# Attention and a gated feed-forward layer on one core: two more head pairs with an unsplit product with v

## The chip, the core and the metric

The kernel runs on one core of a Trainium2 chip. The metric is the device time of one execution in microseconds (us); the figure for a kernel is the median of its runs. The engines are TensorE (PE in the profile, PEld for its weight loads), VectorE (DVE), ScalarE (ACT), GpSimd (POOL) and SyncE (SP), which issues nearly all transfers.

## The reference

For each of 8 batches and 8 heads (576 positions, 64 channels per head) attention is computed with a threshold: scores more than tau below the maximum of their row are dropped. The output of the heads is then fed through two large matrices with a gate between them.

```python
scores = scale * np.matmul(q, k.transpose(0, 1, 3, 2))
thresh = np.max(scores, axis=-1, keepdims=True) - tau
scores = np.where(scores >= thresh, scores, -1000000000.0)
scores = scores - np.max(scores, axis=-1, keepdims=True)
attn = np.exp(scores)
attn = attn / (np.sum(attn, axis=-1, keepdims=True) + 1e-09)
out = np.matmul(attn, v)                 # all heads side by side: x, 4608 x 512
h = x @ w_in                             # 512 -> 2048
g = h * np.tanh(log1p(exp(h)))
return g @ w_out                         # 2048 -> 512
```

## The kernel before, in words

**Tiles, steps, pairs.** Two heads make a *pair*; there are 32 pairs, four to a batch. The 2 x 576 query rows of a pair are nine *tiles* of 128 rows, so there are 288 tiles, numbered g = 0 to 287 over all pairs. One main loop runs over g; a turn of it is called a *step* here. Each engine does its instructions in the order in which this loop writes them (class `InOrder`, whose call is line 93: nearly every row of the profile carries L93 for that reason). Only SP's transfers are ordered by the scheduler.

**What a step does.** In step g, PE computes the scores s of tile g+1 (`begin`). DVE takes the row maximum of tile g (`row_max`, a TENSOR_REDUCE), ACT the exponential e (`exponential`), DVE masks and sums to p (`masked`), POOL normalises p of tile g-1 (`normalise`). PE transposes p of tile g-2 into tp and t (`transposes`); ACT copies the transposed tile g-3 to SBUF. The product with v (`product`) is made once per group of tiles: a pair has four of them, closed by its tiles 1, 4, 6 and 8 (`LAST`), 256 or 320 columns wide; their result y goes to x by ACT (the *gather*). When a pair is done, `split_x` makes xh and xl of it.

**Split and plain.** A float32 product is made on PE either *plain* (operands float32) or *split*: an operand is rounded to the short form fp32r (hi) and the rest is kept as a second operand (lo), and two or three fast matmuls replace the slow one. Pairs below `FULL` (4) have the plain product with v: `values_full`, five chunks `y<-pf,vf` and one gather. Their transposed tiles are copied as they are (`evacuate`: pf), and they take a transposition of the tail t in every tile. Later pairs have the split one: `values`, nine matmuls with hi, lo and tk; ACT rounds tp to hi and the tail to tk, DVE subtracts (`lo_main`, `tail_lo`), POOL splits v, and after the product ACT copies two halves (x, yo), which POOL adds. The first four pairs also have plain scores for their second head (`PLAIN`), the others split scores for both.

**The bookkeeping of the two forms.** In the plain form the transposes of tile g-2 stand early in a step, after the scores, and a product comes four steps after the tile that closes it; its gather stands on ACT one step after its last chunk. In the split form the transposes stand at the end of a step, the product comes five steps after, and its gather stands in the same step. In the first 39 steps the chunks of a plain product are dealt out over steps (`PIECES`: 2 to 4 per step); from then on up to five are issued in a step.

**First matrix product.** From step 42 on PE also runs the product h with w_in of the batch before (`gemm1`), as a stream from which each step takes a written number of matmuls: `MIX_FIRST` for the first batch, beginning with 6, 14, 22, 6, 16, 4, 12, 4, 15, 9, 16, 13 for the steps 42 to 53. Twelve matmuls fill one PSUM bank, which ACT then copies out (`leave`, hst). Banks of h and banks of y come out of one pool of two (`psh`). w_in is decoded from 8-byte words while the first 53 steps run (`Decode`: dec on ACT, DVE and POOL; w1h, w1l). The second product (o) follows the attention.

Of the kernel before, what the change touches and what calls it, by code (L numbers as in the profile page):

```python
# [16 lines left out]
NP = H // 2  # L17
LOADS = ((1, 0, 1, 3, 2, 3, 7, 3, 5, 8), (0, 3, 3, 2, 5, 4, 5, 8, 5, 7), (0, 0, 2, 4, 5, 4, 7, 6, 7, 8))
# [5 lines left out]
ORDER = (0, 0)  # L24
PIECES = (3, 3, 3, 3, 4, 2, 3, 4, 3)
WARM = (24, 2, 10)
FULL = NP
UNV = 54
ONP = 1
ONV = (3, 9, 11, 12, 14, 15, 17, 18, 22)  # L30
# [1 line left out]
PLAIN = (1,)  # L32
# [46 lines left out]
def fv(ap):  # L79
    return ap.bitcast(F32)  # L80
# [78 lines left out]
def attention_moe(tc, q, k, v, tau, w_in, w_out, out):  # L159
# [3 lines left out]
    with ExitStack() as outer:  # L163
# [12 lines left out]
        with ExitStack() as first:  # L176
# [6 lines left out]
            with ExitStack() as att:  # L183
# [31 lines left out]

                def prep(pi):
                    full = pi < FULL
                    plain = PLAIN if full else ()
                    qs, k1, k2 = [], [], []
                    for a in range(2):  # L220
                        kind = F32 if a in plain else F32R
                        qs.append(ops.tile([P, 640], kind, name=f"q{a}"))
                        k1.append(ops.tile([P, S + D], kind, name=f"k1{a}"))
                        k2.append(None if a in plain else ops.tile([P, S + D], kind, name=f"k2{a}"))
                    made = dict(qs=qs, k1=k1, k2=k2, plain=plain)
                    if full:
                        made["vf"] = ops.tile([P, 2, 5, D], F32, name="vf", tag="vs")

                    def part(src, n):
                        r = raw.tile([P, 320], F32, name="r")  # L230
                        nc.sync.dma_start(r[:, :n], src)
                        return r[:, :n]

                    def q_part(c):
                        a, half = divmod(c, 2)
                        sl = slice(half * 320, (half + 1) * 320)
                        at = slice(c * 320, (c + 1) * 320)
                        if a in plain:
                            nc.sync.dma_start(qs[a][:D, sl], q[pi, :D, at])
                            return skip  # L240
                        r = part(q[pi, :, at], 320)

                        def split():
                            nc.scalar.copy(qs[a][:, sl], r)
                            nc.gpsimd.tensor_tensor(qs[a][D:, sl], r[D:], fv(qs[a][D:, sl]), ALU.subtract)

                        return split

                    def k_part(a, c):
                        sl = slice(c * 320, (c + 1) * 320)  # L250
                        if a in plain:
                            nc.sync.dma_start(k1[a][:D, sl], k[pi, :D, a, sl])
                            return skip
                        r = part(k[pi, :, a, sl], 320)

                        def split():
                            nc.scalar.copy(k1[a][:, sl], r)
                            nc.gpsimd.tensor_tensor(k2[a][:, sl], r, fv(k1[a][:, sl]), ALU.subtract)

                        return split  # L260

                    def v_part(a):
                        if full:
                            nc.sync.dma_start(made["vf"][:, a], v[pi, :, a])
                            return skip
                        if a == 0:
                            made["vs"] = ops.tile([P, 2, 5, 2, D], F32R, name="vs")
                        vs = made["vs"]
                        r = part(v[pi, :, a].rearrange("p c d -> p (c d)"), 320)
                        r = r.rearrange("p (c d) -> p c d", d=D)  # L270

                        def split():
                            nc.scalar.copy(vs[:, a, :, a, :], r)
                            nc.gpsimd.tensor_tensor(vs[:, a, :, 1 - a, :], r, fv(vs[:, a, :, a, :]), ALU.subtract)

                        return split

                    loads = [lambda c=c: q_part(c) for c in range(4)]
                    loads += [lambda a=a, c=c: k_part(a, c) for a in range(2) for c in range(2)]
                    loads += [lambda a=a: v_part(a) for a in range(2)]  # L280
                    return made, loads
# [49 lines left out]
                def transposes(g):  # L331
# [7 lines left out]
                    t5 = None  # L339
                    if g < FULL * 9:  # L340
                        t5 = pst.tile([P, P], F32, name="t5")
# [47 lines left out]
                def values_full(r, pt, vf, x):  # L389
                    main, tail = pt.pop(r)  # L390
                    n = WIDTH[r]
                    a = r // 2
                    y = psh.tile([P, 512], F32, name="y", tag="ph")

                    def chunk(c):
                        if c < 4:
                            nc.tensor.matmul(y[:D, :n], vf[:, a, c], main[:, c, :n], start=c == 0, stop=False)
                        else:
                            nc.tensor.matmul(y[:D, :n], vf[:D, a, 4], tail[:D, 0, :n], start=False, stop=True)

                    def gather():
                        nc.scalar.copy(x[a * D:a * D + D, XOFF[r]:XOFF[r] + n], y[:D, :n])

                    return [lambda c=c: chunk(c) for c in range(5)], gather
# [108 lines left out]
                def start_pair(g, pi):  # L513
                    parts, todo = prep(pi)
                    pairs[pi] = dict(ops=parts, pt={})
                    for work, step in zip(todo, LOADS[1 if 2 <= pi < FULL + 2 else pi % 2 * 2]):
                        loads.setdefault(g + step, []).append(work)

                def begin(g):
                    pi, t = divmod(g, 9)  # L520
                    made = pairs[pi]["ops"]
                    tiles[g] = dict(s=scores(t, D if g % 2 == 0 else 0, **made))

                def product(g):
# [4 lines left out]
                    if t in LAST:  # L529
                        if pi < FULL:  # L530
                            some, gather = values_full(LAST[t], pr["pt"], pr["ops"]["vf"], pr["x"])
# [14 lines left out]

                warm_up(WARM[0])
                start_pair(0, 0)
                for step in range(8):
                    for work in loads.pop(step, []):  # L550
                        work()()
                begin(0)
                for g in range(NT + 5):
                    now = [work.pop(0) for work in decoding]
                    decoding = [work for work in decoding if work]
                    if g + 1 < NT:
                        begin(g + 1)
                    ahead = 2 <= g < FULL * 9 + 2
                    lag = 4 if g < FULL * 9 + 4 else 5
                    if lag <= g < NT + lag and g != FULL * 9 + 4:  # L560
                        product(g - lag)
                    if 3 <= g < NT + 3:
                        old = ((g - 3) % 9, *tiles[g - 3]["tp"], pairs[(g - 3) // 9]["pt"])
                        full = g - 3 < FULL * 9
# [6 lines left out]
                        tiles[g - 2]["tp"] = transposes(g - 2)  # L571
                    done = list(ready)
                    ready.clear()
                    for _ in range(5 if g >= FULL * 9 + 3 else PIECES[g % 9]):
                        if pieces:
                            work, then = pieces.pop(0)
                            work()
                            if then:
                                ready.append(then)
# [39 lines left out]
                    if g % 9 == 7 and g // 9 + 2 < NPAIRS:  # L619
                        start_pair(g, g // 9 + 2)  # L620
                    if g == 0:
                        start_pair(-2, 1)
                        loads[0] = loads.pop(-2) + loads[0]
# [17 lines left out]
                    b, step = divmod(g - 6, 36)  # L641
# [54 lines left out]
            work = {}  # L696
# [139 lines left out]
        for c, ds, qs in steps:  # L836
# [3 lines left out]
            g = ready[c]  # L840
# [58 lines left out]
```

## Time and profile before

| | |
|---|---|
| runs | 1384.63, 1387.59, 1375.18 us (median 1384.63) |
| profiled execution | 1382.82 us, its span 1381.0 us |
| PE busy | 1360.2 us (98%) |
| DVE, ACT, POOL busy | 1000.4 (72%), 944.0 (68%), 771.9 us (56%) |
| step 36 begins on DVE, step 56 begins | 126.55 us, 199.60 us |
| first matmul of h | 149.14 us |

The times in the profile are counted from the start of the span. The first three slices of the 40 hold the first four pairs (plain), the next two hold pairs 4 and 5. A matmul's record is longer than the distance to the next one, since matmuls overlap in the engine; distances between starts are used below where work is counted.

### The profile page before, as it was taken

What the parts mean: (1) busy time and instruction counts of PE and PEld (TensorE: products, weight loads), DVE (VectorE), ACT (ScalarE), POOL (GpSimd) and SP (SyncE); (2) the same over time, 40 slices, a digit from 0 to 9 for tenths busy, and PEclk for the clock granted to TensorE, in tenths of its full rate; (3) what the DMA queues carried; (4) which work ended last, traced back from release to release, by engine and by line L of the source; (5) the groups of instructions that cost most, each with busy time, mean ns of one, the idle gap of its engine ahead of it and who ended that gap; (6) DMA issues with size and microseconds to landing.
All of it is one profiled execution on the core that took longest, in us unless ns stands there. A gap on an engine that the chain in (4) does not pass through costs nothing.

```text
span 1381.0 us, 27611 instructions
## 1 busy us (share of the span) xinstructions
PE 1360.2 (98%) x8798; PEld 1228.1 (89%) x8798; DVE 1000.4 (72%) x2976; ACT 944.0 (68%) x2106; POOL 771.9 (56%) x1115
## 2 busy tenths in 40 slices
PE   8999899999999999999999999999999999999999
PEld 5555789999999999999999999999888888888888
DVE  4899999999999999999999999957874332232210
ACT  3778788888888888888888888856555543443210
POOL 3678798788787787887878878733460000000000
PEclk6999899999999999999999999999999999999999
DMA  4334323333233333333333333218655543543310
GB/s 134 87 94 109 114 91 103 103 97 116 89 115 109 98 102 100 98 114 92 115 100 102 107 100 97 82 60 282 202 162 149 159 143 110 145 122 107 92 53 24
DMA packets 126017, 154.64 MB, mean 112 GB/s; under 512 B 23472, under 2 KB 109488, under 8 KB 125872
## 3 DMA queue, kind: packets, MB, share of 16 engines
q1 hardware_dynamic: 124720, 148.16, 35.7%
q10 hardware_dynamic: 1152, 4.72, 0.9%
q8 instruction: 70, 1.15, 0.4%
q14 instruction: 75, 0.61, 0.1%
HBM read 105.64 MB, written 47.19 MB: 111 GB/s over the span
## 4 chain that ended last, share of the span: by engine, by line
PE 91%; DVE 3%; ACT 3%; issue 1%; DMA 1%; POOL 0%; SPq 0%; ACTq 0%; DVEq 0%; POOLq 0%
PE o L848 29%; PE h L93 26%; PE s L93 14%; PE y L93 12%; PE tp L93 9%; PE t L93 1%; DVE st L93 1%; DVE p L93 1%; DVE g L93 1%; DVE dec L93 1%; ACT e L93 1%; DMA g<-w_out 1%; ACT g L93 0%; ACT dec L93 0%; POOL g L93 0%
## 5 line engine op out<-in xcount | busy, mean ns | idle before, releaser
L848 PE MATMUL o<-g,w2h 128*128 128x512 f32 (+1 forms) x1280 | 363.7, 370 | 0.0
L93 PE MATMUL h<-xh,w1h 128*128 128x288 f32 x1024 | 303.0, 296 | 2.7 <-ACT hst L93 1.4
L93 PE MATMUL h<-xl,w1h 128*128 128x288 f32 x1024 | 302.8, 296 | 0.0
L93 PE MATMUL h<-xh,w1l 128*128 128x288 f32 x1024 | 302.7, 296 | 0.0
L93 POOL TENSOR_SCALAR p<-p,st 128x576 f32<-128x576 f32 x288 | 243.7, 846 | 66.9 <-DVE st L93 41.5
L93 PE MATMUL s<-k,q 128*128 128x288 f32 (+1 forms) x1280 | 260.8, 329 | 10.0 <-DVE p L93 8.4
L848 PEld LDWEIGHTS o<-g,w2h 128*128 128x128 f32 x1280 | 231.7, 188 | 41.9
L93 DVE SCALAR_TENSOR_TENSOR p<-s,st,e 128x576 f32<-128x576 f32 x288 | 235.1, 816 | 23.4 <-ACT e L93 13.8
L93 ACT ACTIVATE e<-s,st 128x576 f32<-128x576 f32 x288 | 214.4, 744 | 34.5 <-DVE st L93 28.9
L848 PE MATMUL o<-g,w2l 128*128 128x512 f32 (+1 forms) x640 | 235.8, 368 | 0.0
L93 DVE TENSOR_REDUCE st<-s 128x1 f32<-128x576 f32 x288 | 216.8, 753 | 12.2 <-PE s L93 12.2
L93 PEld LDWEIGHTS s<-k,q 128*128 128x128 f32 (+1 forms) x1280 | 185.5, 192 | 42.1 <-DVE p L93 22.3
L93 DVE TENSOR_TENSOR lo<-tp,hi 128x512 fp32r<-128x512 f32 (+1 forms) x280 | 174.8, 633 | 49.0 <-ACT hi L93 42.4
L93 PEld LDWEIGHTS h<-xh,w1h 128*128 128x128 f32 x1024 | 193.3, 189 | 4.0 <-ACT hst L93 2.0
L93 PEld LDWEIGHTS h<-xh,w1l 128*128 128x128 f32 x1024 | 193.1, 189 | 0.0
L93 PEld LDWEIGHTS h<-xl,w1h 128*128 128x128 f32 x1024 | 193.0, 188 | 0.0
L93 PE MATMUL tp<-ident,p 128*128 128x128 f32 x1152 | 176.7, 276 | 3.5 <-DVE lo L93 2.3
L93 ACT CAST hi<-tp 128x512 fp32r<-128x512 f32 (+1 forms) x280 | 149.8, 546 | 36.0 <-PE tp L93 33.0
L681 DVE TENSOR_TENSOR g<-ht,g 128x1024 fp32r<-128x1024 f32 (+1 forms) x60 | 68.6, 1154 | 136.0 <-ACT g L680 136.0
L93 PEld LDWEIGHTS tp<-ident,p 128*128 128x128 f32 x1152 | 140.4, 142 | 15.2 <-issue 7.6
L848 PEld LDWEIGHTS o<-g,w2l 128*128 128x128 f32 x640 | 120.3, 188 | 21.6
L93 POOL TENSOR_TENSOR x<-x,yo 64x256 f32<-64x256 f32 (+1 forms) x112 | 89.8, 802 | 87.8 <-ACT yo L93 84.6
(87 smaller groups left out, 2189.6 us busy)
## 6 DMA issues: line engine op xcount, KB each, us to landing
hd<-hst SPq DMA_DIRECT2D x56, 576.0 KB, 3.3
r<-q SPq DMA_DIRECT2D x120, 160.0 KB, 2.3
r<-k SPq DMA_DIRECT2D x120, 160.0 KB, 2.3
ht<-hd SPq DMA_DIRECT2D x52, 288.0 KB, 3.2
r<-v SPq DMA_DIRECT2D x56, 160.0 KB, 2.3
dec<-w_in SPq DMA_DIRECT2D x32, 256.0 KB, 2.7
out_t<-ost SPq DMA_DIRECT2D x32, 256.0 KB, 2.9
g<-w_out SPq DMA_DIRECT2D x48, 128.0 KB, 3.2
```

The costliest lines, as they stand in the source:

```text
L93: made = method(*args, **kwargs)
L681: engine.tensor_tensor(gl, ht, fv(gh), ALU.subtract)
L848: nc.tensor.matmul(o[:, :m], a, b, start=n == 0, stop=n == 3 * NF - 1)
```

## The change

`FULL` becomes `NP + 2`, six: pairs 4 and 5 take the plain product with v, the early transposes, the lag of four steps and the later gather. Three uses of the old value are pinned, so that the rest stays as it was: `plain` still holds only for the first four pairs (the scores of pairs 4 and 5 stay split), `LOADS` is chosen as before, and the chunks of a product are issued up to five a step from step 40 on (it was step 39).

```diff
-FULL = NP
+FULL = NP + 2
+WHOLE = 40
...
                     full = pi < FULL
-                    plain = PLAIN if full else ()
+                    plain = PLAIN if pi < NP else ()
...
-                    for work, step in zip(todo, LOADS[1 if 2 <= pi < FULL + 2 else pi % 2 * 2]):
+                    for work, step in zip(todo, LOADS[1 if 2 <= pi < NP + 2 else pi % 2 * 2]):
...
-                    for _ in range(5 if g >= FULL * 9 + 3 else PIECES[g % 9]):
+                    for _ in range(5 if g >= WHOLE else PIECES[g % 9]):
```

What this does to the order of the instructions is shown at two places. First PE around the second product of pair 4. Before, in step 45 (y_2037 is this product, h_2020 the bank of h that is being filled, hi_1803 and lo_1804 the split transposed tile):

```order
L93 MATMUL y_2037<-lo_1804,vs_1363 128x320
L93 MATMUL y_2037<-tk_1805,vs_1363 128x320
L93 MATMUL h_2020<-xh_1437,w1h_96 128x288
L93 MATMUL h_2020<-xl_1438,w1h_96 128x288
L93 MATMUL h_2020<-xh_1437,w1l_97 128x288
L93 MATMUL h_2020<-xh_1776,w1h_96 128x288
L93 MATMUL h_2020<-xl_1777,w1h_96 128x288
L93 MATMUL h_2020<-xh_1776,w1l_97 128x288
```

Now, in step 44 (y_1943 is the same product, pf_1790 its transposed tile, h_1929 and h_1989 two banks of h in a row):

```order
L94 MATMUL tp_1946<-ident_79,p_1866 128x128 x3
L94 MATMUL t5_1951<-ident_79,p_1866 64x128
L94 MATMUL y_1943<-pf_1790,vf_1158 64x320 x4
L94 MATMUL y_1943<-pf_1791,vf_1158 64x320
L94 MATMUL h_1929<-xh_1436,w1l_97 128x288
L94 MATMUL h_1929<-xh_1818,w1h_96 128x288
L94 MATMUL h_1929<-xl_1819,w1h_96 128x288
L94 MATMUL h_1929<-xh_1818,w1l_97 128x288
L94 MATMUL h_1989<-xh_711,w1h_96 128x288
L94 MATMUL h_1989<-xl_712,w1h_96 128x288
```

The product has moved one step ahead, from the step with 6 matmuls of h into the step with 22, and the transposes stand ahead of it. The 22 end one bank (h_1929), fill a second (h_1989) and begin a third.

Second ACT in the same steps. Before, steps 44 and 45 (hst takes a finished bank, x and yo are the gather):

```order
L93 COPY hst_1944<-h_1946 128x288
L93 COPY hst_1944<-h_2006 128x288
L93 CAST hi_1906<-tp_2027 128x4x128
L93 ACTIVATE e_2050<-s_1962,st_2049 128x576
L93 ACTIVATE dec_1882<-dec_1882 128x256
L93 ACTIVATE dec_1882<-dec_1882 128x256
L93 COPY x_1841<-y_2037 64x320
L93 COPY yo_2047<-y_2037 64x320
```

Now, the same two steps:

```order
L94 COPY hst_1927<-h_1929 128x288
L94 COPY hst_1927<-h_1989 128x288
L94 COPY pf_1884<-tp_1946 128x4x128
L94 COPY pf_1885<-t5_1951 64x128
L94 ACTIVATE e_2025<-s_1938,st_2024 128x576
L94 ACTIVATE dec_1864<-dec_1864 128x256
L94 COPY x_1788<-y_1943 64x320
```

The gather of y_1943 stands behind the copies of both banks of h that end in the product's own step, so y's bank is held for the rest of that step, and h_1929 and h_1989 share the other one: the program makes the first matmul of h_1989 wait for the copy out of h_1929, and the first of the third bank for the copy out of h_1989. Before, in these steps, a bank of h waits for the copy of the bank before the last one, or for a gather.

## The prediction

> **What bounds the kernel now.** I read the page first, then a table by stage, then who waited for whom on PE.
>
> ```profile
> span 1381.0 us, 27611 instructions
> PE 1360.2 (98%) x8798; PEld 1228.1 (89%) x8798; DVE 1000.4 (72%) x2976; ACT 944.0 (68%) x2106; POOL 771.9 (56%) x1115
> ```
>
> PE is the bound of the whole. The table by stage says where it isn't; the columns are the length of the stretch, busy time of PE, PEld, DVE, ACT and POOL, then PE's granted clock.
>
> ```profile
> 126.00:150.20 24.20, 20.89 (x101) 14.19 (x100) 22.92 (x80) 19.18 (x49) 20.94 (x25) 0.86 0.37 103
> 150.20:211.20 61.00, 56.07 (x403) 53.34 (x402) 57.90 (x191) 49.57 (x126) 51.15 (x67) 0.97 0.30 95
> 211.20:266.70 55.50, 55.50 (x428) 54.79 (x427) 51.08 (x169) 47.47 (x115) 45.02 (x70) 1.00 0.33 103
> ```
>
> From 211 us on PE is busy without a gap at full clock. In the 85.2 us before that, where pairs 4 and 5 are, it stood still for 24.20 - 20.89 + 61.00 - 56.07 = 8.2 us, and the clock was down. The waits in that stretch (126 to 212 us):
>
> ```profile
> PE s L93 <- DVE p L93: 4.9, 8, 1.1
> PE tp L93 <- DVE lo L93: 2.3, 2, 1.3
> PE tp L93 <- POOL dec L93: 0.9, 1, 0.9
> ```
>
> So DVE, late with p and lo, is what PE waits for. The clock, window by window:
>
> ```profile
> 139.60:143.00 3.40, 1.41 (x10) 0.96 (x9) 2.83 (x8) 3.33 (x9) 2.11 (x4) 1.00 0.35 96
> 143.00:149.80 6.80, 5.80 (x25) 5.08 (x24) 6.71 (x22) 5.69 (x16) 6.80 (x9) 0.50 0.34 93
> 153.20:156.60 3.40, 1.66 (x12) 1.40 (x12) 3.40 (x17) 2.88 (x9) 2.06 (x3) 1.00 0.23 80
> 156.60:160.00 3.40, 3.40 (x17) 3.40 (x16) 3.33 (x11) 1.81 (x5) 2.44 (x3) 0.50 0.24 57
> ```
>
> Twice PE was busy for less than half of 3.4 us (1.41 and 1.66), and each time the next stretch ran at half clock: 6.8 + 3.4 = 10.2 us, which cost 10.2 x 0.5 = 5.1 us of PE's work.
>
> **The change, part by part.** The kernel's end is set by PE from 211 us on, so what counts is when PE has done the same work there: its added work, less the idle time and the slow clock that go, plus the new waits.
>
> *Added work: the product.* These rows of the chain of waits have whole products or parts of them:
>
> ```profile
> 130.70 1.76 PE y L93 x6
> 133.18 1.36 PE y L93 x4
> 136.40 2.44 PE y L93 x10
> 183.90 1.06 PE y L93 x9
> 209.67 1.71 PE h L93 x13
> 228.72 1.33 PE y L93 x9
> ```
>
> A plain chunk leaves two records. The one whole product (136.40, five chunks, 256 wide) took 2.44 us; one of 320 in two parts took 1.76 + 1.36 = 3.12, and 2.44 x 320/256 is 3.05, which I take. The split ones took 1.06 (256) and 1.33 (320). A pair has two of each: 2 x (2.44 + 3.05) = 10.98 now against 2 x (1.06 + 1.33) = 4.78, so +6.2 us. The row of h gives the distance of two of its matmuls, 1.71/13 = 0.13 us.
>
> *Added work: the tails.* Nine transpositions t per pair in place of four or five.
>
> ```profile
> 101.69 0.60 PE L93 MATMUL tp<-ident,p 128*128 128x128 f32 x4
> 102.12 0.27 PE L93 MATMUL t<-ident,p 128*64 128x128 f32 x1
> ```
>
> Four start within 102.12 - 101.69 = 0.43 us, so 0.11 each: 4.5 x 0.11 = 0.5 us a pair. Both together 6.7 us a pair, **+13.4 us** for two pairs. This lies on PE's path wherever PE is dense; it would be free where PE waits anyway, which the next item counts.
>
> *What goes on the other engines.* Per pair DVE loses these, nine tiles' worth of each:
>
> ```profile
> L93 DVE TENSOR_TENSOR lo<-tp,hi 128x512 fp32r<-128x512 f32 x224 | 153.7, 686 | 40.0 <-ACT hi L93 34.7
> L93 DVE TENSOR_TENSOR tk<-t,tk 64x128 fp32r<-64x128 f32 x224 | 64.7, 289 | 5.0
> ```
>
> That is some 9 x (0.69 + 0.29) = 8.8 us a pair, about 1 us per step, which is what DVE was late by. ACT loses yo and the rounding of v, POOL the split of v and four additions. None of it is on PE. The load of v goes straight to its tile on SP and waits there for pair 2's and 3's v to be done, with loads of q, k and w_in queued behind; the first four pairs have the same, and v is needed some nine steps later: I cost it at nothing, hidden by those steps, and at one late step, 3 us, if not.
>
> *What PE gets back.* All of the 8.2 us idle and the 5.1 us of clock, 13.3 us. The idle time in the records is short by what a record outlasts the distance to the next (0.30 - 0.13 = 0.17 us for h, from the page's 296 ns), once per pause: 11 pauses, 1.8 us. So at most **15.1 us**, and not less than about 8 if DVE's lateness stays in part.
>
> *Why it might stay in part.* Until step 42 PE has no h, and DVE still has the decoding. The maxima, one per step:
>
> ```profile
> 126.55 0.75 DVE L93 TENSOR_REDUCE st<-s 128x1 f32<-128x576 f32 x1
> 129.19 0.76 DVE L93 TENSOR_REDUCE st<-s 128x1 f32<-128x576 f32 x1
> 131.74 0.75 DVE L93 TENSOR_REDUCE st<-s 128x1 f32<-128x576 f32 x1
> 145.97 0.74 DVE L93 TENSOR_REDUCE st<-s 128x1 f32<-128x576 f32 x1
> ```
>
> Six steps (36 to 41) took 19.4 us; at DVE's floor of 2.55 they would take 15.3, and PE's own work in them is about 16.8 (seven sets of scores at 4 x 0.13, six of transposes at 5 x 0.11, about 3.7 products' worth of chunks at 2.4 to 3.05 in parts). I take 17.5 us, hence 0.7 us idle. Besides, DVE's decoding stood still for 2.29 us while POOL ran three additions or subtractions in a row, and only the first of these three goes:
>
> ```profile
> 150.47 2.29 DVE L93 SCALAR_TENSOR_TENSOR dec<-dec 128x256 uint32<-128x256 uint32 x1
> ...
> 150.28 0.73 POOL L93 TENSOR_TENSOR x<-x,yo 64x256 f32<-64x256 f32 x1
> 150.97 0.81 POOL L93 TENSOR_TENSOR xl<-x,xh 128x288 fp32r<-128x288 f32 x1
> 151.74 0.73 POOL L93 TENSOR_TENSOR w1l<-dec,w1h 128x256 fp32r<-128x256 f32 x1
> ```
>
> So 2.29 - 0.73 = 1.5 us may be left of it, of which PE sees half or so. Idle that stays: **1.5 us** (0 to 3).
>
> *New waits.* With y's bank held until the next step's gather, two banks of h in a row share one bank of PSUM. The program has seven such places with no other matmul between (two in step 44, one in each of 46, 48, 50, 53 and 57). PE then waits for the copy:
>
> ```profile
> 204.81 0.29 PE L93 MATMUL h<-xh,w1l 128*128 128x288 f32 x1
> ...
> 205.14 0.40 ACT L93 COPY hst<-h 128x288 f32<-128x288 f32 x1 [0.64 <-PE h L93]
> ```
>
> From the start of a bank's last matmul to the end of its copy 205.54 - 204.81 = 0.73 us, one more hand-over like the 0.04 between them, less the ordinary 0.13: 0.64 us. Queued behind are all of that step's h, and the next scores. 7 x 0.64 = **4.5 us**; nothing if ACT's copy could be hidden, which the order rules out, and twice that if ACT comes late to it.
>
> *Sum.* 13.4 - 15.1 + 1.5 + 4.5 = **+4.3 us**. On the profiled execution of 1382.8 us that is 1387.1; its time was 1.8 us below the median of the runs, where it makes 1388.9. I predict 1388.
>
> [...]
>
> **The rivals.**
>
> *Forecast: added work and new waits slightly outweigh what comes back.* +4.3, from about +1 to +8. Chance 0.52.
>
> *DVE's relief comes through in full.* The seven copies find ACT waiting and PE's pauses shrink, the 15.1 come back, and idle time stays at nothing: 13.4 - 15.1 + 2 x 0.64 = about 0, so 1382 to 1384. For: PE waits for DVE alone in this stretch. Against: the order of the banks. Chance 0.22.
>
> *The clock goes down again (slower).* Place: steps 42 to 57, where steps alternate between 22 matmuls of h with a product (about 6.5 us of PE) and 6 without. After a long step, the short one needs p, which needs e, which on ACT stands behind hst and pf; if PE is then busy for less than about half of 3.4 us (as in the two rows), the next 3.4 us run at half clock and cost 1.7. If the old stretches stay, +5.1: 1394. If each of the seven long steps brings one, 7 x 1.7 = 11.9 more: 1400. It decides from pauses of about 1.7 us in 3.4; those that I count are 0.64. Chance 0.14.
>
> *DVE stays late until the decoding ends.* Only 8 of the 15.1 come back: +11.4, 1396. Against: 1 us less per step. Chance 0.08.
>
> *A real gain.* More than 15.1 us isn't there to be had in this stretch, and past 211 us there is no gap at all; only if plain chunks cost less in one run than 2.44 us. Chance 0.04: below 1371.
>
> **How the numbers follow.** A measurement of this kernel can tell about 1% (13.8 us) from no change; its own three runs lie 12 us apart. Faster by over 1%: 0.04, the last case. Slower by over 1% needs 1398: part of the third and fourth cases, 0.09. Within 1%: 0.87. The range takes the first two cases, most of the third and fourth, and the spread of the runs: 1378 to 1398.
>
> **What would show it.** Right: in 126 to 160 us the granted clock at 1.00; first matmul of h near 145 us instead of 149; waits of PE for ACT's hst, about seven of 0.5 to 0.7 us; no wait for lo before 195 us; DVE idle where it had none; the point at which PE is dense (the transpose of tile 57, 211.2 us before) at about 214 to 216. Wrong: if that point comes before 210 us, the added work was hidden; if the clock shows 0.50 again after 145 us, the third case holds; if PE waits for p as long as before, the fourth.

## The result, and the profile after

The changed kernel took 1394.07 us (median of 20 runs, 1385.26 to 1399.31), the kernel before on the same chip 1381.25 us (20 runs, 1373.52 to 1387.59). The ratio is 1.0092, 95% interval 1.0071 to 1.0114: slower by some 12.7 us, about 0.9%. The forecast was 1388 in a range of 1378 to 1398; the time lies in the range and within 1%, but of the 12.7 us the sum had only 4.3. Range and 1% hold narrowly, and by luck rather than by the sum: 12.7 us on the 1384.6 from which the forecast was counted make 1397, a us from the end of the range, and the interval reaches over 1%. The profiled execution took 1395.36 us.

The page after, first lines:

```profile
span 1393.6 us, 27559 instructions
PE 1371.9 (98%) x8815; PEld 1225.1 (88%) x8815; DVE 983.3 (71%) x2936; ACT 937.1 (67%) x2094; POOL 763.7 (55%) x1103
```

PE is busy for 1371.9 - 1360.2 = 11.7 us longer, and DVE for 17 us less. The table by stage (length, then busy time of PE, PEld, DVE, ACT and POOL, PE's granted clock, the share of the DMA engines, GB/s):

```profile
126.00:150.20 24.20, 23.10 (x131) 15.46 (x130) 23.24 (x84) 20.85 (x56) 22.10 (x28) 1.00 0.45 126
150.20:211.20 61.00, 54.89 (x328) 41.10 (x328) 33.83 (x124) 35.58 (x94) 36.41 (x47) 1.00 0.26 81
211.20:266.70 55.50, 54.27 (x404) 51.67 (x403) 47.68 (x157) 43.76 (x106) 41.85 (x64) 1.00 0.30 90
```

The clock is 1.00 all through, and DVE, which was busy for 57.90 of the 61 us from 150 us on, now has work for 33.83. But PE still stands still, for 61.00 - 54.89 = 6.1 us against 4.9 before, and for some more past 211 us. These windows lie at fixed times, and the kernel after has come less far in them. Over the same tiles (34 to 62, see below) DVE went from 93.65 of 100.01 us to 77.68 of 111.56, first the kernel before, then after:

```profile
127.32:227.33 100.01, 92.09 (x623) 83.02 (x622) 93.65 (x315) 82.60 (x208) 84.88 (x110) 0.95 0.34 105
126.88:238.44 111.56, 103.11 (x640) 80.04 (x639) 77.68 (x273) 76.39 (x198) 76.19 (x100) 1.00 0.31 94
```

The waits of PE after (stretch from 126.9 to 238.5 us):

```profile
PE h L94 <- ACT hst L94: 3.4, 7, 0.5
PE s L94 <- DVE p L94: 1.5, 2, 0.8
PE tp L94 <- POOL q L94: 1.0, 2, 0.5
PE tp L94 <- POOL p L94: 0.8, 1, 0.8
PE tp L94 <- POOL w1l L94: 0.7, 1, 0.7
PE tp L94 <- ACT pf L94: 0.5, 2, 0.3
PE tp L94 <- POOL xl L94: 0.5, 1, 0.5
```

DVE's lo and POOL's dec are gone. ACT's hst has come, and so have five rows for the early transposes tp, under as many names: 3.5 us in this view, more between starts, since a record outlasts the distance to the next (for a transpose 0.27 us to 0.11).

**Where the time is lost.** The start of the transposes of a tile marks the same point in both kernels. After minus before, it is -0.44 us at tile 34, -5.1 at tile 40 (145.12 us), +11.14 at tile 57 (222.36 us against 211.22), and it stays at +11.14 at tile 80 and +10.9 at tile 287. These 11 us come between tiles 34 and 57. So from here on I use **the stretch** from the transposes of tile 34 to those of tile 62: 100.01 us before, 111.57 after. A second profile of the changed kernel gave 111.58, though its whole time was 6.0 us longer, so one profile is taken to be enough. That the stretch of the other kernels repeats as well is not shown; it is least sure where a piece of it runs at half clock, as before the change and in some of the variants.

In the stretch the distance between the starts of successive PE matmuls splits the time: the ordinary distance of each kind where PE is dense (0.13 us for h, 0.11 for a transpose, 0.27 and 0.21 for a record of a plain chunk), single pauses of over 0.2 us on top, and a rest of many small pieces (slow clock, changes from one kind to the other). Worked out from the starts in the trace, in us:

| | stretch | ordinary | pauses ahead of h | ahead of tp | ahead of s | rest |
|---|---|---|---|---|---|---|
| before | 100.0 | 81.4 | 0 | 3.8 (3) | 6.7 (10) | 8.2 |
| after | 111.6 | 92.2 | 4.55 (7) | 4.5 (7) | 2.1 (3) | 8.2 |

The pauses ahead of h are as forecast. Those ahead of tp are new. Two rows of PE after and four of ACT, on two timelines, show one of them (start, length, in brackets the idle time before):

```profile
188.43 0.69 PE L94 MATMUL s<-k,q 128*128 128x288 f32 x4
189.77 0.63 PE L94 MATMUL tp<-ident,p 128*128 128x128 f32 x4 [0.65 <-POOL w1l L94]
```

```profile
188.63 0.40 ACT L94 COPY hst<-h 128x288 f32<-128x288 f32 x1 [0.18 <-PE h L94]
188.93 0.38 ACT L94 COPY pf<-tp 128x256 f32<-128x256 f32 x1
189.19 0.21 ACT L94 COPY pf<-t 64x64 f32<-64x64 f32 x1
189.30 0.38 ACT L94 COPY pf<-tp 128x256 f32<-128x256 f32 x1
```

tp neither reads nor writes w1l, which the view names. It reads p and takes the one bank that tp has, and this is free when ACT has copied the tile before to pf: at 189.30 + 0.38 = 189.68, and tp begins at 189.77. Six of the seven pauses end 0.09 to 0.15 us after such a copy. In four of them, this one among them (2.8 of the 4.5 us), the copy stands on ACT right behind hst, and hst behind the last matmul of a bank of h. In the other two it stands behind ACT's rounding and decoding, at 141.37 us, before the first h, and at 171.87 us:

```profile
170.84 0.40 ACT L94 CAST w1h<-dec 128x256 fp32r<-128x256 f32 x1
171.14 0.58 ACT L94 COPY pf<-tp 128x512 f32<-128x512 f32 x1
```

The seventh and longest, at 147.97 us, ends 0.05 us after POOL has made p: there tp waits for what it reads. This is a reading of the order and of times; the experiments put it to the test.

### The profile page after: what moved, and what is told of

It is laid out like the page before. It is cut to its first block, busy times and chain, and to the rows that moved or that the text cites. A ratio compares the mean times of both kernels' runs of the same rounds, so it can differ in the third digit from the quotient of the medians.

```text
span 1393.6 us, 27559 instructions
## 1 busy us (share of the span) xinstructions
PE 1371.9 (98%) x8815; PEld 1225.1 (88%) x8815; DVE 983.3 (71%) x2936; ACT 937.1 (67%) x2094; POOL 763.7 (55%) x1103
## 4 chain that ended last, share of the span: by engine, by line
PE 84%; DVE 4%; ACT 3%; DMA 3%; POOL 2%; issue 2%; SPq 1%; ACTq 0%; POOLq 0%; DVEq 0%
PE h L94 25%; PE o L849 23%; PE s L94 13%; PE y L94 12%; PE tp L94 9%; PE t L94 1%; DMA g<-w_out 1%; DVE st L94 1%; DVE g L94 1%; DVE p L94 1%; POOL w2l L157 1%; DMA hd<-hst 1%; ACT e L94 1%; DMA ht<-hd 1%; SPq L718 1%
## 5 line engine op out<-in xcount | busy, mean ns | idle before, releaser
L94 DVE TENSOR_TENSOR lo<-tp,hi 128x512 fp32r<-128x512 f32 (+1 forms) x260 | 162.3, 633 | 49.4 <-ACT hi L94 42.6
L94 ACT CAST hi<-tp 128x512 fp32r<-128x512 f32 (+1 forms) x260 | 139.1, 545 | 33.4 <-PE tp L94 30.5
L677 ACT ACTIVATE ht<-ht 128x1024 f32<-128x1024 f32 (+1 forms) x60 | 60.2, 1004 | 117.5 <-DMA ht<-hd 114.5
```

The lines of the kernel that those rows point to most:

```text
L94: made = method(*args, **kwargs)
L677: nc.scalar.activation(ht, ht, AF.Mish)
```

## The experiments

All times of the stretch are from one profile each; ratios are to the kernel before, run beside it on the same chip.

**The three new waits, one at a time.** The first three edits each take away what makes one wait. Theory A: each wait costs what it shows, and taking it away brings that back. Theory B: another wait takes its place.

*Gather in the product's own step*, so that y's bank is free at once and no two banks of h share one:

```diff
-                                ready.append(then)
+                                (now_done if g >= WHOLE else ready).append(then)
...
-                    for gather, closed in done:
+                    for gather, closed in done + now_done:
```

> The gather of y stands in the product's own step instead of the next one (from step 40 on); nothing else moves. Theory A (waits): the seven places where two banks of h share one bank are gone, and with them 7 x (0.65 + 0.11) = 5.3 us; against it ACT now stands still for y in the long steps, which may give 1 to 2 us back: 3 to 5 us less than the changed kernel, ratio to before about 1.006. Theory B (the added PE work alone sets the time, other waits take the place of these): less than 1.5 us, ratio 1.008 to 1.010.

Ratio 1.0091 (1.0058 to 1.0124), stretch 111.01. The waits of PE:

```profile
PE tp L94 <- POOL k L94: 2.5, 2, 1.3
PE s L94 <- DVE p L94: 2.4, 4, 1.0
PE tp L94 <- POOL p L94: 1.0, 1, 1.0
```

The seven waits for hst, 4.55 us, are gone, and 0.6 us came back: pauses ahead of tp grew from 4.5 to 7.0 us and ahead of s from 2.1 to 3.5. ACT now stands still for y instead:

```profile
147.54 0.42 ACT L94 COPY x<-y 64x320 f32<-64x320 f32 x1 [3.24 <-PE y L94]
```

*The transposes late*, as in the split pairs, so that ACT has the whole step to empty the bank of tp:

```diff
-                    ahead = 2 <= g < FULL * 9 + 2
+                    ahead = 2 <= g < NP * 9 + 2
```

> The transposes of pairs 4 and 5 stand at the end of a step again, behind h, as they did before the change; products and gathers stay. Theory A: the waits of the transposes for ACT's copy of the tile before, which stands behind hst (4.7 us in all between scores and transposes), are covered by h: 3 to 4 us less than the changed kernel, ratio about 1.0065; the bank waits stay. Theory B: less than 1.5 us.

Ratio 1.0064 (1.0035 to 1.0093), stretch 110.25. The waits:

```profile
PE s L94 <- DVE p L94: 3.5, 7, 0.7
PE h L94 <- ACT hst L94: 3.4, 7, 0.5
```

No pause ahead of tp is left, which agrees with the reading above, and pauses ahead of s grew from 2.1 to 4.8 us. Only 1.3 us came back.

*The lag of five steps from step 40 on*, which puts each product back into the step where it stood before:

```diff
-                    lag = 4 if g < FULL * 9 + 4 else 5
-                    if lag <= g < NT + lag and g != FULL * 9 + 4:
+                    lag = 4 if g < WHOLE else 5
+                    if lag <= g < NT + lag and g != WHOLE:
```

> From step 41 on a product comes five steps after its tile instead of four, so that it falls into the steps with 4 to 9 matmuls of h, as before the change; gather and transposes stay. Theory A: banks alternate again (5.3 us) and the steps are more even, 5 to 8 us less than the changed kernel, ratio 1.003 to 1.0055. Theory B: PE has the same work in another order, less than 1.5 us.

Ratio 1.0058 (1.0026 to 1.0090), stretch 107.80: 3.8 us back, the most of the three. Theory A falls for the first two, and the third is between. The changed kernel itself, run again beside them:

> The changed kernel itself, beside the three edits below on one chip: ratio to before 1.007 to 1.012 as measured before. It is the base from which the edits are read.

It gave 1.0113 (1.0072 to 1.0153) and the 111.58 us told above. The intervals of the three edits all overlap with this one, so it is the stretch that tells them apart, and the ratios do not.

**All at once, and the work alone.** Theory C: hst, pf and e in a row on ACT make one chain that causes the pauses. Theory D: what counts is PE's added work, which lies on the path in full. Four kernels: the three edits together; the kernel as changed but with three of the five chunks of each product of pairs 4 and 5 left out (two plain chunks a product remain); as changed, with the copies pf of pairs 4 and 5 on DVE; and the three edits with pf on DVE.

```diff
-                    return [lambda c=c: chunk(c) for c in range(5)], gather
+                    return [lambda c=c: chunk(c) for c in keep], gather
...
+                        elif on_dve:
+                            evacuate(*old, nc.vector.tensor_copy)
```

The first diff is of the second kernel (keep is 0 and 4 for pairs 4 and 5), the other of the third and fourth, where `on_dve` holds for these two pairs' tiles and the copy stands where DVE's `lo_main` stands in a split pair.

> The three edits together: gather in the product's step, late transposes, lag of five steps; only the product itself is still plain for pairs 4 and 5, in the schedule of the split form. Read on the stretch between the transposes of tiles 34 and 62 (before 100.0 us, changed 111.6, lag five alone 107.8). Theory C (PE's pauses come from one chain on ACT, hst, then pf, then e, which each schedule meets somewhere else): 104 to 107 us, not back at 100. Theory D (the added PE work is what counts and all of it is on the path): 111 less the waits, which would need all pauses gone to come below 106.

Ratio 1.0010 (0.9981 to 1.0039), stretch 101.52. Its row over the whole stretch, and all its waits there:

```profile
118.17:219.69 101.52, 99.55 (x640) 80.05 (x639) 76.89 (x273) 78.05 (x198) 76.35 (x100) 1.00 0.34 103
```

```profile
PE tp L94 <- ACT pf L94: 1.1, 1, 1.1
PE s L94 <- DVE p L94: 0.8, 1, 0.8
```

The three edits brought 0.6, 1.3 and 3.8 us, together 5.7 if they added up; made at once they bring 10.05. That is more than C gave; D had room below 106 only with all pauses gone, and of 11.15 us of pauses 2.5 are left. PE is busy for 99.55 of 101.52 us, with the full added work still in it (92.2 us of ordinary distances).

> The changed kernel with three of the five chunks of every product of pairs 4 and 5 left out (their contribution to x is missing), the order otherwise the same. PE has 12 x 0.54 + 12 x 0.43 = 11.6 us less to do. Theory D: the stretch loses 11 to 12 us (about 100). Theory C: the pauses grow where the product covered ACT's chain, 6 to 9 us (103 to 106).

Stretch 101.19, ratio 0.9989 (0.9956 to 1.0021). The work left out is 92.2 - 80.6 = 11.6 us, and 10.4 came back; the pauses stayed (PE's wait for hst is still 3.4 us in seven), and those ahead of tp grew by 1.0 us, which is most of what is missing. So the pauses were not slack that PE's work could hide in, nearly as D has it.

> The changed kernel with the plain copies pf of pairs 4 and 5 moved from ACT to DVE (where lo stood before the change). Theory C: transposes no longer wait behind hst (4.7 us), and e comes 0.8 us sooner after hst; bank waits stay: the stretch loses 4 to 6 us (106 to 107.5). Theory D: less than 1 us. A third way: DVE becomes late again as before the change, and nothing is won or some is lost.

Stretch 112.74, ratio 1.0097 (1.0057 to 1.0137). ACT is relieved of 11 us in the stretch, DVE has as much more, and nothing comes back:

```profile
PE tp L94 <- DVE pf L94: 4.2, 6, 2.1
PE h L94 <- ACT hst L94: 3.4, 7, 0.5
```

Here the view names pf itself as what tp waits for, in six pauses, and all eight of over 0.2 us end 0.15 us after such a copy: tp does wait for its bank. Ahead of tp 6.0 us are lost between starts, against 4.5 as changed, so what C gave does not come and nothing is won, as the third way had it. This does not clear ACT's row in the changed kernel, though, for on DVE the copy has a queue ahead of it too, the row maximum and what follows from it:

```profile
163.08 0.76 DVE L94 TENSOR_REDUCE st<-s 128x1 f32<-128x576 f32 x1 [0.28 <-PE tp L94]
164.13 0.67 DVE L94 COPY pf<-tp 128x512 f32<-128x512 f32 x1
164.72 0.27 DVE L94 COPY pf<-t 64x128 f32<-64x128 f32 x1
```

```profile
164.95 0.63 PE L94 MATMUL tp<-ident,p 128*128 128x128 f32 x4 [0.47 <-DVE pf L94]
```

> The three edits of the schedule and pf on DVE together. Theory C: 102 to 105 us for the stretch, ratio to before 1.002 to 1.004. If DVE is what limits (it has the load of lo again): no better than the three edits alone.

Stretch 103.76, ratio 1.0024 (0.9989 to 1.0059): with the three edits made, moving pf to DVE makes it 2.2 us worse, by pauses and by a piece at half clock (149.6 to 153.0 us).

**Two at a time.** Theory E: the early transposes are the wait that holds. Theory F: the lag is what counts. The diffs are the ones above, two each.

> Gather in the product's own step and the lag of five from step 40 on; the early transposes of pairs 4 and 5 stay. The stretch from the transpose of tile 34 to that of tile 62 took 111.6 us as changed, 111.0 with the gather alone, 107.8 with the lag alone, 101.5 with all three edits. Theory E (the early transposes are the wait that holds: what stands behind them on PE waits for ACT's copy of the tile before): 105.5 to 108, with some 4.5 us lost ahead of the transposes, though the waits for the bank of h are gone. Theory F (the lag is what counts, since it puts the product back into the steps with few matmuls of h): 102 to 104.

> Gather in the product's own step and the transposes late; the lag of four stays. Same stretch. Theory E: 102 to 104. Theory F: 106 to 109, since the product still stands in the steps with 22, 16 and 15 matmuls of h and PE then waits for p in the short steps (as with late transposes alone, 3.5 us).

> Lag of five from step 40 on and the transposes late; the gather stays one step later. Same stretch. Theory E: 102 to 104, the waits for banks of h being about 1 to 2 us with the lag of five. Theory F: the same 102 to 104, so this run tells only whether the gather matters: if it does, 104 to 106 with waits of h for hst or x.

Measured, with the pauses of over 0.2 us from the starts and the time at half clock, whose cost is in the rest of the stretch. The three pairs of edits ran once each (1383.28, 1378.55 and 1380.14 us), so they have no ratio.

| edits made | stretch | ahead of h | ahead of tp | ahead of s | at half clock |
|---|---|---|---|---|---|
| none (as changed) | 111.6 | 4.55 | 4.5 | 2.1 | 0 |
| gather | 111.0 | 0 | 7.0 | 3.5 | 0 |
| late | 110.3 | 4.55 | 0 | 4.8 | 0 |
| lag | 107.8 | 1.2 | 4.5 | 1.6 | 3.4 |
| gather, lag | 108.8 | 0 | 5.4 | 1.5 | 6.8 |
| gather, late | 105.8 | 0 | 0.2 | 5.4 | 0 |
| lag, late | 106.1 | 3.15 | 0.4 | 1.3 | 3.4 |
| all three | 101.5 | 0 | 1.3 | 1.2 | 0 |

E and F both fall: neither edit is the one that matters. Gather with lag came at 108.8, near E's 105.5 to 108 and far from F's 102 to 104. It is even a us above the lag alone, but 6.8 us of it ran at half clock: with half of that time taken off, the most that it can have cost, this pair comes to 105.4 (an estimate), the lag alone to 106.1 and lag with late to 104.4. Gather with late came at 105.8, nearer to F's 106 to 109 than to E's 102 to 104. Lag with late came at 106.1, outside what both gave at first, and at the end of F's second case (104 to 106, the gather matters). Each pair leaves the one wait that the third edit removes: tp without late, s without lag, h without gather. With the gather or the late transposes alone the pause moves to another of these three places, and 0.6 and 1.3 us come back; with the lag alone it does not move, the pauses fall by 3.85 us and 3.8 come back.

**One pair instead of two.** With all three edits and `FULL = NP + 1`, so that pair 5 is split again (the tails of a split pair are handled two tiles at a time, which here begins with a single one).

> Only pair 4 takes the plain product (five pairs in all), with gather, lag and transposes as in the kernel with all three edits; pair 5 is split as before the change. Same stretch; before the change it took 100.0 (81.4 of work, 18.6 of pauses and slow clock), with two pairs and all three edits 101.5 (92.1 of work, 9.3 of pauses). Theory C (the relief of DVE in pair 4 alone is enough to end its lateness): work 86.8, pauses 7 to 9, so 94 to 96, and the time 4 to 6 us below before, 0.996. Theory D (DVE is late again in pair 5 until the decoding ends): pauses 11 to 14, so 98 to 101, and the time within 2 us of before.

Ratio 0.9985 (0.9950 to 1.0020), stretch 100.01: equal to before. D was right. Ordinary distances are 86.9 us, as C and D both had it, but the pauses come back in pair 5, the largest in one place:

```profile
192.74 0.79 PE L94 MATMUL s<-k,q 128*128 128x288 f32 x4 [2.57 <-DVE p L94]
```

```profile
188.01 0.76 DVE L94 TENSOR_TENSOR lo<-tp,hi 128x256 fp32r<-128x256 f32 x2 [0.62 <-ACT hi L94]
188.69 2.46 DVE L94 TENSOR_SCALAR dec<-dec 128x256 f32<-128x256 f32 x1
191.16 0.67 DVE L94 TENSOR_TENSOR tk<-t,tk 64x128 fp32r<-64x128 f32 x3
191.85 0.82 DVE L94 SCALAR_TENSOR_TENSOR p<-s,st,e 128x576 f32<-128x576 f32 x1
```

p, which PE waits for, stands on DVE behind one instruction of the decoding that took 2.46 us; the shortest of its kind took 0.27. So none of the versions tried beats the kernel before by more than the measurement can tell.

## Why the prediction was right or wrong, point by point

- *Added work, +13.4: right to about a us.* A product of 320 took 2.98 us (3.05 taken), one of 256 took 2.44 as taken; rows of the chain of waits of after:

```profile
151.66 2.98 PE y L94 x10
162.88 2.98 PE y L94 x10
172.60 2.44 PE y L94 x10
```

  In the starts it is 92.2 - 81.4 = 10.8 us of ordinary distances, and 3.6 us more of small gaps around plain chunks (4.6 against 1.0 before): 14.4. That nearly all of it is on the path was shown by the left-out chunks: 10.4 back for 11.6.
- *What comes back, -15.1: about a us too much.* Of the 18.6 us that stood over ordinary distances before, 4.55 are a rest that after has too (its 8.16 without the 3.6 of plain chunks), so 14.05 came back. Half a us of the excess was counted twice: in the 10.2 us at half clock PE was busy for 5.80 + 3.40 = 9.2, so at a granted clock of 0.50 it cost 4.6 us and not 5.1 (an estimate), and the rest is idle time already.
- *The clock:* 1.00 in 126 to 160 us and on to the end of the stretch, as forecast. The rival of a clock that goes down again did not happen here; it did in the stretch of five variants, for 3.4 or 6.8 us each, in the kernel with one plain pair after a pause of 2.57 us.
- *First h near 145:* it came at 145.58 us.

```profile
145.58 0.38 PE L94 MATMUL h<-xh,w1h 128*128 128x288 f32 x1
```

- *Seven hand-overs of a bank at 0.64, +4.5:* seven, 0.65 each between starts, 4.55. The mechanism and the size were right; that removing it alone would bring it back was not said, and is not so (0.6 us).
- *No wait for lo before 195 us, DVE idle:* right. The rival in which DVE stays late gave +11.4, near the time that came, but not by its mechanism: DVE was busy for 33.83 of 61 us and p cost 2.1 us, not what was left of 15.1.
- *Idle that stays, +1.5 (0 to 3):* 2.1 us ahead of s, inside its range.
- *New waits: this is the step that failed.* Its list had the hand-overs of h and nothing for the transposes, which were costed at PE's 0.11 us each. The change also puts them ahead of the product and of h, right behind the scores, and there they lost 4.5 us in seven pauses: in six they wait for the one bank of tp until ACT has copied the tile before to pf, in four of these with hst right ahead of that copy, and in one they wait for p. Everything that PE has in that step is queued behind. The row was within reach: hst is in the order of the change, right ahead of pf.
- The sum with what was measured: 14.4 - 14.05 + 4.55 + 4.5 + 2.1 = 11.5 us, against the stretch's 111.57 - 100.01 = 11.56. Of the 7.3 us that the forecast was short, 4.5 are the pauses ahead of tp, 0.6 those ahead of s, 1.0 the plain chunks, 1.1 what came back.
- *Dense point at 214 to 216:* 222.36, for the same reasons. *DVE's relief in full (about 0)* is what the three edits together show: +1.5 in the stretch, ratio 1.0010. It was a fair price for the change, but not for the order of instructions that came with it.

What stays open: why a pause moves from one place to the next was read from the waits, not measured by itself. One reading fits: steps with many matmuls of h and steps with few alternate, a short one lasts as long as its way from scores over max, e, p, transposes and copy, and only work put into the short steps (the lag of five does that) is covered. No run changed the numbers of h per step. In the second matrix product PE lost another 1.6 us to waits for g, of which the kernel before shows none; I did not follow this up.

## What to carry to other kernels

When an instruction is moved earlier on the busiest engine, price its wait as well as its work: look for what has to free its bank, and what stands ahead of that on the other engine. Relief of the engine waited for is worth only what the next wait in the loop leaves of it; three waits here cost 4.5, 4.5 and 2.1 us, and one edit against them brought 0.6 to 3.8 us, two 2.8 to 5.8, and all three 10. If single edits give little, try them together before calling the waits harmless.

## What the runs showed of the hardware

**The time at half clock at the start goes with a difference of some 10 us.** The stretch of the changed kernel repeats to 0.01 us in two profiles, and yet runs of one kernel lie up to 17 us apart. The profiles differ in how long PE is at half clock at the start. The kernel before and the one with all three edits, which are alike so far into the program, from 20 to 30 us:

```profile
20.00:30.00 10.00, 10.00 (x30) 6.03 (x29) 5.21 (x24) 4.22 (x11) 3.36 (x4) 0.50 0.09 22
```

```profile
20.00:30.00 10.00, 10.00 (x51) 6.02 (x50) 7.76 (x34) 7.23 (x20) 5.86 (x7) 1.00 0.18 50
```

PE was busy for 10.00 of 10.00 us in both rows, and in the first the clock stayed at 0.50. The kernel before and the changed one ran at half clock for 27.3 us at the start, and the transposes of tile 34 begin at 127.32 and 126.88 us. With all three edits it was some 10 us (granted 0.89 and 0.60 from 0 to 10 and 10 to 20 us), and they begin at 118.17; with one plain pair some 34 us (0.63, 0.50, 0.50 and 0.66 in the tens from 10 to 50 us), and they begin at 130.88. The edits do not account for all of it, since the second profile of the changed kernel is 6.0 us longer with the same stretch. This is why single times say little here and the ratios are made from several runs.

**The clock fell after 3.40 us with some work in them.** In the kernel with one plain pair, around the pause of 2.57 us:

```profile
189.20:192.60 3.40, 0.97 (x8) 0.73 (x7) 3.34 (x7) 1.26 (x4) 1.79 (x3) 1.00 0.14 40
194.00:195.00 1.00, 1.00 (x6) 1.00 (x6) 1.00 (x3) 1.00 (x3) 0.96 (x2) 0.50 0.00 0
```

PE was busy for 0.97 of 3.40 us, and soon after ran at half clock, from 193.6 to 197 us or so. As in the rows of the kernel before (1.41 and 1.66 us), the window was partly busy. The changed kernel, with its pauses of 0.65 us, kept the clock at 1.00 from 37.5 to 1392.5 us.

Not every stretch as empty was followed by a fall. The kernel with pf on DVE kept its clock through this one:

```profile
147.60:151.00 3.40, 1.05 (x7) 0.77 (x7) 3.40 (x15) 1.19 (x3) 2.54 (x4) 1.00 0.62 183
```

PE was busy for 1.05 us in it, less than in both rows of the kernel before, and from 126.56 to 239.30 us the clock of this kernel was 1.00.

In the kernel before the clock changed at 143.0, 149.8, 156.6 and 160.0 us, and so stayed at one value for 6.83, 6.83 and 3.41 us. Cut from these changes on into windows of 3.41 us, from 60 to 1370 us, its profile has PE busy for 1.42 and 1.67 us in the two windows ahead of the falls, and for at least 1.98 us in every other window at full speed. The profile of the changed kernel, cut in the same way from its change at 37.5 us, has no fall and no window with less than 1.89 us. These are two profiles; why the stretch with 1.05 us of work was not followed by a fall was not shown.

**Some of DVE's decoding took longer while POOL was busy.** One of these instructions took 2.46 us. The tile's view in the kernel with one plain pair (shortest, median and longest in ns), and POOL at that time, running one instruction after another:

```profile
L94 DVE TENSOR_SCALAR dec<-dec x64: 272/330/2458, 25.9 to 194.2; 128x256 f32<-128x256 f32 x32, 128x256 uint32<-128x256 uint32 x32
```

```profile
188.61 0.75 POOL L94 TENSOR_TENSOR dec<-dec 128x256 uint32<-128x256 uint32 x1
189.33 0.83 POOL L94 TENSOR_SCALAR p<-p,st 128x576 f32<-128x576 f32 x1
190.12 0.87 POOL L94 TENSOR_TENSOR k<-r,k 128x320 fp32r<-128x320 f32 x1
```

In the kernel before, twelve instructions of this row with POOL busy for at most 0.57 of their time took 0.27 to 0.29 us; 37 with POOL busy all the while took 0.28 to 1.05, half of them 0.47 or more. DVE's row maxima took 0.74 to 0.76 us either way. What draws the decoding out was not shown; no run took POOL's work away.
